# The second product of C11 in seven narrow products of its own, and k^T v in two halves through one buffer

## The chip, the cores and the metric

The kernel runs on one core of a Trainium2 chip. Its metric is the device time of one execution in microseconds. A run's time is compared with the median of three runs of the kernel before.

## The reference

An attention block without softmax, and then a feed-forward block with a squared ReLU, all in float32:

```python
# q, k, v: (8, 8, 576, 64)
kv  = einsum('bhsd,bhse->bhde', k, v)
out = einsum('bhsd,bhde->bhse', q, kv)
rms = sqrt(mean(out * out, axis=-1, keepdims=True) + 1e-6)
x   = (out / rms * g_norm).transpose(0, 2, 1, 3).reshape(4608, 512)
h   = x @ w_in                        # w_in (512, 2048)
r   = maximum(h, 0)
y   = (s * (r * r) + b) @ w_out       # w_out (2048, 512)
```

## The kernel before

The 4608 tokens are worked off in nine units u = 0 to 8 of 512 tokens. A unit is four chunks c of 128 tokens: the chunk's q is transposed (`turn`), multiplied by k^T v (`product`), normed (`norm`) and transposed back into xT (`turn_x`, 512 features in four blocks of 128 partitions, by 512 tokens).

**First product, x @ w_in.** For u >= 1 it is done by the Strassen-Winograd scheme at one level: features and tokens are each cut in two, so that a 2x2 block product takes seven products instead of eight. The blocks of the tokens' side are in xT (c, column halves of TB = 256 tokens) and their sums in `xs` (`x_sums`); those of the weights are in `wa`, `wb` and their sums in `ws` (`sums_w_in`). It is done in four steps s = 0 to 3; one step (`mm1(u, s)`) makes 256 columns of w_in by the upper and the lower half. Within a step the product i is four matmul calls (`mm1_product`: b over two blocks of 128 output features, c over two blocks of 128 input features), each of 256 token columns. In float32 a call is two PE instructions. The names say the product and the bank: x1, x6, x5, x3 are added up in one PSUM bank "x", y7 and y4 in a bank "y", z2 in a bank "z". C11 = product 1 + product 2: x1 is kept by ACT in r1 (line 569), and the DVE adds the bank of z2 to it (line 230) and squares its ReLU (line 524). C22 comes from x5 and y7 in the same way, x3 gives a21 (ReLU on ACT, line 600, square on DVE, line 603), y4 gives a12. The results, `ga`, are pairs of steps in one tile, `g_pair`, whose blocks the second product takes as weights.

**Second product, times w_out.** Unit 0 and 1 do it by one level of the scheme. From u = 2 on four of its products are done by a second level (`second_level`), again seven for eight, with matmuls of 128 columns; its banks are "x" or "y", "z" and "y", one tile each. Its weights come from DRAM into a ring of seven buffers, which `pump` fills by DMAs of SP (lines 645, 648).

**The order is written out by hand.** Each engine runs its instructions in the order in which the program names them. The slots of the steps are listed (x1 of a step, x3 of the step before, z2, y4 of the step before, x6, y7, x5), and beside certain slots stand other things: the sums of the weights of steps 1 to 3 in unit 1 (n = 1, 3, 5), k^T v of one batch (`kv_product`, units 1 to 6, n = 12), the load of the next k and v (`load_kv`, n = 14).

**Loads.** The DMAs of the units are issued by SP (but for two stores at the end). At the start of unit u, `loads(u)` issues the q of unit u + 1 (`load_q`: 34, 48, 32, 64, 48, 48, 32 DMAs in units 1 to 7, as a chunk's rows lie in one or two batches; line 155). `load_kv` (line 103) loads half of a batch's heads by four DMAs of 288 KB, two for k and two for v; both halves have a buffer of their own (bufs=2). `kv_product` (line 360) runs 144 instructions of 64x64 matmuls into two PSUM tiles kv_ps; four copies bring these to bd_kv (lines 373, 375).

PSUM has eight banks: two "t" (kv, transposes), one for the attention ("x" of ps_a), two "x", two "y", one "z". A bank holds 128 partitions by 512 float32 words, the whole of a tile [128, 2, 256].

Of the kernel before, what the change touches and what calls it, by code (L numbers as in the profile page):

```python
# [16 lines left out]
def kernel(  # L17
# [9 lines left out]
    moe_b: bass.AP,  # L27
    out: bass.AP,
):

# [211 lines left out]
    def sums_w_in(s):  # L244
# [12 lines left out]

        return s12, s34

    def w_in_of(i, s, b, c):  # L260
        return {
            1: lambda: wa[s][:, c, b],
            2: lambda: wa[s][:, KH + c, b],
            3: lambda: ws[s][:, 2, c, b],
            4: lambda: wb[s][:, KH + c, b],
            5: lambda: ws[s][:, 0, c, b],
            6: lambda: ws[s][:, 1, c, b],
            7: lambda: wb[s][:, c, b],
        }[i]()
# [75 lines left out]
        for _ in range(n):  # L345
            matmul(ps[:, 0, :P], ident, ident, True, True)

    def kv_product(b):


        ps = [ps_t.tile([P, 2, D], FP32, name="kv_ps", tag="t") for _ in range(2)]
        for i in range(2):
            if b == 0:
                warm((18, 7)[i])
            kv = kv_in.pop((b, i))
            for j in range(R):
                for l in range(2):
                    for r in range(2):
                        rows = slice(r * HB, r * HB + HB)
                        nc.tensor.matmul(  # L360
                            ps[r][l * HB : l * HB + HB, i, :],
                            lhsT=kv[rows, 0, l, j, :],
                            rhs=kv[rows, 1, l, j, :],
                            start=(j == 0),
                            stop=(j == R - 1),
                        )
        for r in range(2):
            for l in range(2):
                ls = slice(l * HB, l * HB + HB)
                to = bd_kv[b % 2][ls, 2 * r : 2 * r + 2, ls].rearrange("p i (c e) -> p i c e", c=KC)  # L370
                src = ps[r][ls].rearrange("p i (e c) -> p i c e", c=KC)
                if b == 0 and l == 1:
                    nc.vector.tensor_copy(out=to, in_=src)
                else:
                    nc.scalar.copy(to, src)
# [109 lines left out]
    def x_sums(u):  # L485
# [12 lines left out]

        return t12, t34

    def x_of(i, u, c):
        if i <= 3:
            c, col = (c, slice(0, TB)) if i == 1 else (KH + c, slice(0, TB) if i == 2 else slice(TB, 2 * TB))
            return xT[u][:, c, col]
        return xs[u, i][:, c, :]
# [5 lines left out]
    def bank_of(key, tag, bufs=2):  # L511
        bank[key] = ps_f.tile([P, 2, TB], FP32, name=f"{tag}_ps", tag=tag, bufs=bufs)
        return bank[key]

    def mm1_product(i, u, s, ps, first):
        for b in range(2):
            for c in range(KH):
                matmul(
                    ps[:, b, :], w_in_of(i, s, b, c), x_of(i, u, c),
                    first and b == 0 and c == 0, c == KH - 1,  # L520
                )
# [4 lines left out]
    def g_tile(name, s):  # L526
        if s % 2 == 0:
            g_pair[name, s // 2] = gp.tile([P, 2, 2, TB], FP32, name=name, tag=name)
        ga[name, s] = g_pair[name, s // 2][:, s % 2]
        return ga[name, s]  # L530
# [32 lines left out]
    def mm1(u, s):  # L563

        st = {}

        def keep(name, src, tag):
            st[name] = rp.tile([P, 2, TB], FP32, name=name, tag=tag)
            nc.scalar.copy(st[name], src)  # L569

        def x1():
            st["x"] = bank_of("x", "x")
            mm1_product(1, u, s, st["x"], True)
            keep("r1", st["x"], "ra")

        def z2():
            ps = bank_of("z", "z", 1)
            mm1_product(2, u, s, ps, True)
            t = g_tile("a11", s)
            add(t, ps, st["r1"])  # L580
            relu_sq(t)

        def x6():
            mm1_product(6, u, s, st["x"], False)
            keep("r2", st["x"], "rb")

        def y7():
            st["y"] = bank_of("y", "y")
            mm1_product(7, u, s, st["y"], True)

        def x5():
            mm1_product(5, u, s, st["x"], False)
            keep("r4", st["x"], "ra")
            t = g_tile("a22", s)
            add(t, st["y"], st["r4"])
            relu_sq(t)

        def x3():
            mm1_product(3, u, s, st["x"], False)
            nc.scalar.activation(g_tile("a21", s), st["x"], AF.Relu)  # L600

        def x3_square():
            nc.vector.tensor_mul(ga["a21", s], ga["a21", s], ga["a21", s])  # L603

        def x3_s1():
            g_tile("s1", s)
            g_s1(s)

        def x3_s3():
            sub(ga["a21", s], ga["a11", s], ga["a21", s])  # L610

        def y4():
            mm1_product(4, u, s, st["y"], False)
            add(g_tile("a12", s), st["y"], st["r2"])

        def y4_square():
            relu_sq(ga["a12", s])

        return dict(
            x1=x1, z2=z2, x6=x6, y7=y7, x5=x5, x3=x3, x3_square=x3_square, x3_s1=x3_s1,  # L620
            x3_s3=x3_s3, y4=y4, y4_square=y4_square,
        )

# [30 lines left out]
    def mm2(u, step=None, att=None):  # L656
# [281 lines left out]
            product_q[c]()  # L938
            norm[c]()

        def sums_ahead():
            p1["sums"]()
            turn[0]()
            turn[1]()

# [73 lines left out]
            y4_of(1, 4)  # L1019
            pump(2)  # L1020

        return sums_ahead, all_of_it


    NU = FC // 2
# [1 line left out]
    def tc_late():  # L1027
        convp.release()
        late["ring"] = ctx.enter_context(tc.tile_pool(name="ringp", bufs=7, side="right"))
        late["sub"] = ctx.enter_context(tc.tile_pool(name="subp", bufs=5, side="right"))  # L1030
        late["tmp"] = ctx.enter_context(tc.tile_pool(name="tmpp", bufs=4, side="right"))
        late["kv"] = ctx.enter_context(tc.tile_pool(name="kvp", bufs=2, side="right"))

    blocks = [i for s in range(NS) for i in (2 * s, NU + 2 * s)]
    blocks += [FC + 2 * s for s in range(2 * NS)]
# [91 lines left out]
    def side_of(u):  # L1127

        if u + 1 >= U:
            return None  # L1130
        turn, product, norm, turn_x, _ = zip(*(attention(c) for c in range(4 * u + 4, 4 * u + 8)))
        if u > 1:
            sums = lambda: [sums() for sums in x_sums(u + 1)]
            return turn, product, norm, turn_x, [sums]
        product = [whole(*steps) for steps in zip(product, norm)]
        side = {
            2: [turn[0]],
            3: [product[0]],
            4: [turn[1]],
            5: [turn_x[0], product[1]],  # L1140
            6: [turn[2]],
            7: [turn_x[1], product[2]],
            8: [turn[3]],
            9: [turn_x[2], product[3]],
            11: [turn_x[3]],
            12: [lambda: [sums() for sums in x_sums(u + 1)]],
        }
        if u == 0:
            side = {
                6: [lambda: kv_product(1)],  # L1150
                7: [turn[0]],
                8: [product[0], turn[1]],
                9: [turn_x[0], product[1], turn[2]],
                10: [turn_x[1], product[2], turn[3]],
                11: [turn_x[2], product[3]],
                12: [turn_x[3], lambda: [sums() for sums in sums_w_in(0)]],
                13: side[12],
            }
        return side
# [24 lines left out]
    for u in range(U):  # L1184
# [9 lines left out]
            for name in ("y4", "y4_square"):  # L1194
                a[name]()

        slots = []
        for s, a in enumerate(steps):
            slots.append(a["x1"])
            if s:  # L1200
                slots.append(partial(x3, steps[s - 1]))
            slots.append(a["z2"])
            if s:
                slots.append(partial(y4, steps[s - 1]))
            slots += [a["x6"], a["y7"], a["x5"]]
        if u == 0:
            first_unit()
        side = side_of(u)
        second = mm2(u, steps[-1], side) if u > 1 else mm2(u)
        for n, slot in enumerate(slots):  # L1210
            slot()
            if u > 1 and n == len(slots) - 2:
                second[0]()
            if u == 1 and n in (1, 3, 5):
                for sums in sums_w_in((n + 1) // 2):
                    sums()
            if u in kv_due and n == 12:
                kv_product(kv_due[u])
            elif u + 1 in kv_due and n == 14:
                for i in range(2):  # L1220
                    load_kv(kv_due[u + 1], i, late["kv"], tag="kv")
        if u > 1:
            second[1]()
            continue
        for n, slot in enumerate(second):
            slot()
# [18 lines left out]
                step()  # L1245
        if u == 0:
            tc_late()
            for i in range(2):
                load_kv(kv_due[1], i, late["kv"], tag="kv")
            pump(7)  # L1250


# [28 lines left out]
```

## Time and profile before

| what | value |
| --- | --- |
| runs | 952.93, 953.19, 955.08 us, median 953.19 |
| profiled execution | 956.6 us, of which the span of the core is 954.8 |
| granted TensorE clock | 0.997 of full |
| PE, DVE, ACT busy | 939.9 us (98%), 611.3 us (64%), 194.5 us (20%) |
| one unit, from u = 3 to 4 | 101.4 us (from 350.53 to 451.89 us) |
| z2 of all units | 256 instructions of 256 columns |
| kv_ps of all batches | 1152 instructions, 64x64 |
| HBM read and written | 125.8 and 24.1 MB |

The page calls an engine busy between the start and the end of an instruction. Matmuls are pipelined and their ends modelled, so the start of one group to the start of the next says what it costs. In the timeline the columns are start, duration, engine, line, operation, output tile and inputs, shapes and count, and in brackets the idle time of the engine just before and the instruction that ended it. PEld is the load of a matmul's weights, which runs beside the matmul before it. SPq is the issue of DMAs.

### The profile page before, as it was taken

What the parts mean: (1) busy time and instruction counts of PE and PEld (TensorE: products, weight loads), DVE (VectorE), ACT (ScalarE), POOL (GpSimd) and SP (SyncE); (2) the same over time, 40 slices, a digit from 0 to 9 for tenths busy, and PEclk for the clock granted to TensorE, in tenths of its full rate; (3) what the DMA queues carried; (4) which work ended last, traced back from release to release, by engine and by line L of the source; (5) the groups of instructions that cost most, each with busy time, mean ns of one, the idle gap of its engine ahead of it and who ended that gap; (6) DMA issues with size and microseconds to landing.
All of it is one profiled execution on the core that took longest, in us unless ns stands there. A gap on an engine that the chain in (4) does not pass through costs nothing.

```text
span 954.8 us, 17222 instructions
## 1 busy us (share of the span) xinstructions
PE 939.9 (98%) x7102; PEld 839.9 (88%) x7102; DVE 611.3 (64%) x1100; ACT 194.5 (20%) x366; POOL 6.7 (1%) x18
## 2 busy tenths in 40 slices
PE   6999999999999999999999999999999999999997
PEld 6888888888889998999889988989899989998997
DVE  1779768475447854686368744884478557864673
ACT  2674132211111112111211212121211111111100
POOL 2000000000000000000000000000000000000000
PEclk9999999999999999999999999999999999999999
DMA  9588929587735666365437554566225541662063
GB/s 216 192 310 230 309 69 260 107 249 253 210 69 140 181 189 138 76 201 159 128 81 200 185 159 84 159 197 181 32 81 180 184 87 42 202 176 68 20 223 100
DMA packets 131709, 151.09 MB, mean 158 GB/s; under 512 B 76592, under 2 KB 89136, under 8 KB 131504
## 3 DMA queue, kind: packets, MB, share of 16 engines
q1 hardware_dynamic: 128528, 148.22, 54.1%
q10 hardware_dynamic: 2784, 1.77, 0.8%
q8 instruction: 56, 0.92, 0.4%
q14 instruction: 21, 0.17, 0.1%
q0 software_dynamic: 320, 0.00, 0.0%
HBM read 125.83 MB, written 24.12 MB: 157 GB/s over the span
## 4 chain that ended last, share of the span: by engine, by line
PE 95%; DMA 2%; DVE 1%; ACT 1%; issue 0%; SPq 0%; ACTq 0%; DVEq 0%
PE x_ps L91 49%; PE y_ps L91 32%; PE z_ps L91 9%; PE x_ps L422 3%; PE kv_ps L360 2%; DMA w_raw<-in_moe_w_in_dram 1%; DMA kv_sb<-in_k_dram 1%; PE qT_ps L401 0%; DVE xn L441 0%; DVE xT L465 0%; ACT xT L471 0%; ACT w_raw L210 0%; ACT w_raw L205 0%; SPq L103 0%; DVE wb L225 0%
## 5 line engine op out<-in xcount | busy, mean ns | idle before, releaser
L91 PE MATMUL x_ps<-w_sb,a 128*128 128x256 f32 (+1 forms) x600 | 130.9, 371 | 0.0
L569 ACT COPY r<-x_ps 128x512 f32<-128x512 f32 x96 | 56.2, 585 | 332.4 <-PE x_ps L91 325.6
L91 PEld LDWEIGHTS x_ps<-w_sb,a 128*128 128x128 f32 x600 | 108.6, 190 | 15.2 <-issue 1.6
L91 PE MATMUL y_ps<-xs,wb 128*128 128x256 f32 x512 | 121.0, 379 | 0.0
L91 PE MATMUL x_ps<-xs,ws 128*128 128x256 f32 x512 | 120.9, 379 | 0.0
L230 DVE TENSOR_TENSOR a<-y_ps,r 128x512 f32<-128x512 f32 x64 | 44.1, 688 | 102.1 <-ACT r L569 96.4
L91 PEld LDWEIGHTS x_ps<-xs,ws 128*128 128x128 f32 x512 | 97.3, 190 | 13.2
L91 PEld LDWEIGHTS y_ps<-xs,wb 128*128 128x128 f32 x512 | 96.7, 190 | 12.9
L91 PE MATMUL x_ps<-xT,wa 128*128 128x256 f32 x384 | 89.6, 380 | 0.1
L91 PE MATMUL y_ps<-w_sb,sub 128*128 128x128 f32 x728 | 89.3, 275 | 0.0
L91 PEld LDWEIGHTS y_ps<-w_sb,sub 128*128 128x128 f32 x728 | 86.8, 192 | 1.3 <-DVE r L671 0.2
L91 PEld LDWEIGHTS x_ps<-xT,wa 128*128 128x128 f32 x384 | 72.3, 190 | 10.2 <-ACT xT L471 0.5
L91 PE MATMUL y_ps<-w_sb,a 128*128 128x128 f32 (+1 forms) x472 | 70.0, 294 | 0.0
L524 DVE SCALAR_TENSOR_TENSOR a<-a 128x512 f32<-128x512 f32 x96 | 66.4, 691 | 3.1
L91 PEld LDWEIGHTS y_ps<-w_sb,a 128*128 128x128 f32 x472 | 63.7, 191 | 4.1 <-issue 1.4
L603 DVE TENSOR_TENSOR a<-a 128x512 f32<-128x512 f32 x32 | 22.1, 689 | 61.0 <-ACT a L600 61.0
L91 PE MATMUL x_ps<-xT,ws 128*128 128x256 f32 x256 | 61.1, 382 | 0.0
L91 PE MATMUL z_ps<-xT,wa 128*128 128x256 f32 x256 | 60.5, 379 | 0.0
L91 PE MATMUL x_ps<-w_sb,s 128*128 128x256 f32 x256 | 59.1, 384 | 0.0
L91 PEld LDWEIGHTS x_ps<-w_sb,s 128*128 128x128 f32 x256 | 47.4, 190 | 8.4 <-issue 2.6
L91 PEld LDWEIGHTS z_ps<-xT,wa 128*128 128x128 f32 x256 | 48.6, 190 | 6.6
L91 PEld LDWEIGHTS x_ps<-xT,ws 128*128 128x128 f32 x256 | 47.6, 190 | 6.3
(126 smaller groups left out, 1060.4 us busy)
## 6 DMA issues: line engine op xcount, KB each, us to landing
w_sb<-w SPq DMA_DIRECT2D x140, 512.0 KB, 4.4
kv_sb<-in_k_dram SPq DMA_DIRECT2D x30, 288.0 KB, 4.8
kv_sb<-in_v_dram SPq DMA_DIRECT2D x30, 288.0 KB, 7.3
w_raw<-in_moe_w_in_dram SPq DMA_DIRECT2D x8, 1024.0 KB, 7.9
w_raw<-in_moe_w_out_dram SPq DMA_DIRECT2D x8, 1024.0 KB, 5.2
w_sb<-w SPq DMA_DIRECT2D x28, 256.0 KB, 2.8
out_dram<-o SPq DMA_DIRECT2D x104, 64.0 KB, 1.7
q_sb<-in_q_dram SPq DMA_DIRECT2D x144, 32.0 KB, 2.2
```

What stands on the lines that cost most here:

```text
L91: nc.tensor.matmul(o, lhsT=lhsT, rhs=rhs, start=start, stop=stop, skip_group_check=True)
L230: nc.vector.tensor_tensor(out=o, in0=a, in1=b, op=ALU.add)
L360: nc.tensor.matmul(ps[r][l * HB : l * HB + HB, i, :], lhsT=kv[rows, 0, l, j, :], rhs=kv[rows, 1, l, j, :], start=(j == 0), stop=(j == R - 1),)
L422: nc.tensor.matmul(ps[32 * p : 32 * p + 32, w, :], lhsT=st["qT"][:, p, 32 * w : 32 * w + 32], rhs=bd_kv[(b if w < 2 else b1) % 2][:, p, :] ...
L524: nc.vector.scalar_tensor_tensor(t, t, 0.0, t, ALU.max, ALU.mult)
L569: nc.scalar.copy(st[name], src)
L603: nc.vector.tensor_mul(ga["a21", s], ga["a21", s], ga["a21", s])
```

## The change

For u >= 1 product 2 of the first product (A12 B21, the z2 of two steps) is made by the scheme once more, over two steps d at a time: `mm1_twice` runs seven products of two matmul calls of 128 token columns, where z2 had four calls of 256 columns a step. x1 is copied by ACT straight into a11, and the seven results are added there by the DVE. Their banks "x" and "y" are the two halves of the z tile, "z" is a tile of ps_a. The sums for it are made from xT (`x21_sums`, for each unit) and from wa (`sums_w12`, once, partly in place). The order of the steps is written for pairs. `kv_product` is called for one half in the first pair of a unit and for the other in the second, and one buffer serves both: the second half is loaded after the product of the first, and the first half of the next batch after the product of the second. The turns of the first two q chunks (u > 1) come earlier, among the products of the second pair.

```diff
+    def sums_w12(s):
+        w12[s] = late["w"].tile([P, 3, P], FP32, name=f"w12_{s}")
+        s1, s2, s4 = (w12[s][:, i] for i in range(3))
+        add(s1, w12_at(s, 1, 0), w12_at(s, 1, 1))
+        sub(s2, s1, w12_at(s, 0, 0))
+        sub(w12_at(s, 1, 0), w12_at(s, 0, 0), w12_at(s, 1, 0))
+        sub(s4, w12_at(s, 0, 1), s2)
...
-    def kv_product(b):
...
-        ps = [ps_t.tile([P, 2, D], FP32, name="kv_ps", tag="t") for _ in range(2)]
-        for i in range(2):
+    def kv_product(b, halves=(0, 1)):
...
+        if halves[0] == 0:
+            kv_ps[b] = [ps_t.tile([P, 2, D], FP32, name="kv_ps", tag="t") for _ in range(2)]
+        ps = kv_ps[b]
+        for i in halves:
...
+        if halves[-1] == 0:
+            return
...
+    def x21_sums(u):
+        x21 = xs[u, 21] = late["w"].tile([P, 4, P], FP32, name="xs_21")
+        sub(x21[:, 0], x21_of(1, 2, u), x21_of(1, 1, u))
+        sub(x21[:, 1], x21_of(2, 2, u), x21[:, 0])
+        sub(x21[:, 2], x21_of(2, 2, u), x21_of(1, 2, u))
+        sub(x21[:, 3], x21_of(2, 1, u), x21[:, 1])
...
             mm1_product(1, u, s, st["x"], True)
-            keep("r1", st["x"], "ra")
-
-        def z2():
-            ps = bank_of("z", "z", 1)
-            mm1_product(2, u, s, ps, True)
-            t = g_tile("a11", s)
-            add(t, ps, st["r1"])
-            relu_sq(t)
+            nc.scalar.copy(g_tile("a11", s), st["x"])
...
+    def mm1_twice(u, d):
+
+        t = {}
+
+        def go(m, bank, first=False):
+            x = xs[u, 21][:, (5, 6, 7, 4).index(m)] if m > 3 else x21_of(*((1, 1), (2, 1), (2, 2))[m - 1], u)
+            for e in range(2):
+                matmul(t[bank][:, e], w12_of(m, 2 * d + e), x, first and e == 0, True)
+
+        def to(b, n, bank):
+            o = g_pair["a11", d][:, :, b, n * P : n * P + P]
+            add(o, o, t[bank])
+
+        def m1():
+            ps = bank_of("z", "z", 1)
+            t["x"], t["y"] = (ps[:, i].rearrange("p (e n) -> p e n", e=2) for i in range(2))
+            go(1, "x", True)
+            to(0, 0, "x")
+
+        def m2():
+            t["z"] = ps_a.tile([P, NP, P], FP32, name="z12_ps", tag="x")[:, :2]
+            go(2, "z", True)
+            to(0, 0, "z")
+
+        def m6():
+            go(6, "x")
+            to(1, 0, "x")
+
+        def m7():
+            go(7, "y")
+
+        def m5():
+            go(5, "x")
+            to(1, 1, "x")
+            to(1, 1, "y")
+
+        def m3():
+            go(3, "x")
+            to(0, 1, "x")
+
+        def m4():
+            go(4, "y")
+            to(1, 0, "y")
+            relu_sq(g_pair["a11", d].rearrange("p s b t -> p (s b t)"))
...
-        late["kv"] = ctx.enter_context(tc.tile_pool(name="kvp", bufs=2, side="right"))
+        late["w"] = ctx.enter_context(tc.tile_pool(name="latep", bufs=1, side="right"))
+        late["kv"] = ctx.enter_context(tc.tile_pool(name="kvp", bufs=1, side="right"))
...
-            sums = lambda: [sums() for sums in x_sums(u + 1)]
+            sums = lambda: [sums() for sums in (*x_sums(u + 1), lambda: x21_sums(u + 1))]
...
+        def kv_half(i):
+            kv_product(kv_due[u], (i,))
+            if i == 0:
+                load_kv(kv_due[u], 1, late["kv"], tag="kv")
+            elif u + 1 in kv_due:
+                load_kv(kv_due[u + 1], 0, late["kv"], tag="kv")
+
...
+        for d in range(NS // 2 if u > 0 else 0):
+            a, b = steps[2 * d : 2 * d + 2]
+            m = mm1_twice(u, d)
+            if u == 1 and d == 0:
+                x21_sums(1)
+                sums_w(1, 0, 1)
+            a["x1"]()
+            if d:
+                x3(steps[2 * d - 1])
+                y4(steps[2 * d - 1])
+            b["x1"]()
+            m[1]()
+            a["x6"]()
+            if d and u > 1:
+                second["turns"]()
+            m[2]()
+            m[6]()
+            a["y7"]()
+            m[7]()
+            m[5]()
+            a["x5"]()
+            if d == 0 and u == 1:
+                sums_w(2)
+            m[3]()
+            m[4]()
+            a["x3"]()
+            if u in kv_due:
+                kv_half(d)
+            for name in ("x3_square", "x3_s1", "x3_s3"):
+                a[name]()
+            y4(a)
+            if u == 1 and d == 0:
+                sums_w(3, 2, 3)
+            b["x6"]()
+            b["y7"]()
+            if d and u > 1:
+                second["sums"]()
+            b["x5"]()
...
-            for i in range(2):
-                load_kv(kv_due[1], i, late["kv"], tag="kv")
+            load_kv(kv_due[1], 0, late["kv"], tag="kv")
```

`sums_w(s, *more)` runs `sums_w_in(s)` and then `sums_w12` for each of `more`.

More of the change, by code (lines that the diff above doesn't have):

```diff
@@ L258, in sums_w_in, with w12_at, w12_of @@
         return s12, s34
+    w12 = {}
+    def w12_at(s, b, c):
+        return wa[s][:, KH + c, b]
+    def sums_w12(s):
[5 more added lines that the diff above has]
+        sub(s4, w12_at(s, 0, 1), s2)
+    def w12_of(m, s):
+        if m in (5, 6, 3):
+            return w12[s][:, (5, 6, 3).index(m)]
+        return w12_at(s, *{1: (0, 0), 2: (0, 1), 4: (1, 1), 7: (1, 0)}[m])
     def w_in_of(i, s, b, c):
@@ L346, in warm @@
             matmul(ps[:, 0, :P], ident, ident, True, True)
-    def kv_product(b):
-        ps = [ps_t.tile([P, 2, D], FP32, name="kv_ps", tag="t") for _ in range(2)]
-        for i in range(2):
+    kv_ps = {}
+    def kv_product(b, halves=(0, 1)):
[3 more added lines that the diff above has]
+        for i in halves:
             if b == 0:
@@ L499, in x_sums, with x21_of @@
         return t12, t34
+    def x21_sums(u):
[4 more added lines that the diff above has]
+        sub(x21[:, 3], x21_of(2, 1, u), x21[:, 1])
+    def x21_of(k, n, u):
+        return xT[u][:, KH + k - 1, n * P - P : n * P]
     def x_of(i, u, c):
@@ L619, in mm1 @@
         return dict(
-            x1=x1, z2=z2, x6=x6, y7=y7, x5=x5, x3=x3, x3_square=x3_square, x3_s1=x3_s1,
+            x1=x1, x6=x6, y7=y7, x5=x5, x3=x3, x3_square=x3_square, x3_s1=x3_s1,
             x3_s3=x3_s3, y4=y4, y4_square=y4_square,
         )
+    def mm1_twice(u, d):
[32 more added lines that the diff above has]
+            relu_sq(g_pair["a11", d].rearrange("p s b t -> p (s b t)"))
+        return {1: m1, 2: m2, 3: m3, 4: m4, 5: m5, 6: m6, 7: m7}
     ring = {}
@@ L939, in attend, with turns @@
             norm[c]()
-        def sums_ahead():
-            p1["sums"]()
+        def turns():
             turn[0]()
@@ L1020, in all_of_it @@
             pump(2)
-        return sums_ahead, all_of_it
+        return {"turns": turns, "sums": p1["sums"], "rest": all_of_it}
     NU = FC // 2
@@ L1145, in side_of @@
             11: [turn_x[3]],
-            12: [lambda: [sums() for sums in x_sums(u + 1)]],
+            12: [lambda: [sums() for sums in x_sums(u + 1)], lambda: u and x21_sums(u + 1)],
         }
@@ L1195, in y4, with sums_w @@
                 a[name]()
[L1197 to L1205, printed above, removed]
+        side = side_of(u)
+        second = mm2(u, steps[-1], side) if u > 1 else mm2(u)
+        def sums_w(s, *more):
+            for sums in sums_w_in(s):
+                sums()
+            for s in more:
+                sums_w12(s)
@@ L1206 @@
+        def kv_half(i):
[4 more added lines that the diff above has]
+                load_kv(kv_due[u + 1], 0, late["kv"], tag="kv")
         if u == 0:
             first_unit()
[L1208 to L1219, printed above, removed]
-                for i in range(2):
-                    load_kv(kv_due[u + 1], i, late["kv"], tag="kv")
+        for d in range(NS // 2 if u > 0 else 0):
[36 more added lines that the diff above has]
+            b["x5"]()
@@ L1222 @@
         if u > 1:
-            second[1]()
+            second["rest"]()
             continue
@@ L1247 @@
             tc_late()
-            for i in range(2):
-                load_kv(kv_due[1], i, late["kv"], tag="kv")
+            load_kv(kv_due[1], 0, late["kv"], tag="kv")
             pump(7)
```

## The prediction

> **What bounds the kernel now.** I read the page's busy times first, then the waits of TensorE (PE), then the timeline in the units u >= 1, where all of the change but its first load lies.
>
> ```profile
> PE   939.9 (98%) x7102; PEld 839.9 (88%) x7102; DVE 611.3 (64%) x1100; ACT 194.5 (20%) x366; POOL 6.7 (1%) x18
> ...
> PE 95%; DMA 2%; DVE 1%; ACT 1%; issue 0%; SPq 0%; ACTq 0%; DVEq 0%
> ```
>
> PE is the bound, and the list of its waits holds 2.0 us of waiting for kv data and some single waits in unit 0: from unit 1 on, PE has no gap. So every column of matmul that is saved counts in full, and so does every new wait of PE. The price of a column comes from the starts of consecutive groups (durations overlap, starts do not):
>
> ```profile
> 296.52 1.05 PE L91 MATMUL x_ps<-w_sb,a 128*128 128x128 f32 x8
> 297.41 1.06 PE L91 MATMUL z_ps<-w_sb,a 128*128 128x128 f32 x8
> ...
> 350.53 1.89 PE L91 MATMUL x_ps<-xT,wa 128*128 128x256 f32 x8
> 352.26 1.89 PE L91 MATMUL z_ps<-xT,wa 128*128 128x256 f32 x8
> 353.99 1.89 PE L91 MATMUL x_ps<-xs,ws 128*128 128x256 f32 x8
> ```
>
> Four calls (eight instructions) of 256 columns take 1.73 us, four of 128 columns 0.89 us. The narrow ones cost 0.1116 us an instruction against half of 0.2158: 3% worse per column.
>
> **1. The second product.** It goes from 2 x 1.727 = 3.454 us a pair of steps to 7 products x 4 instructions x 0.1116 = 3.125 us: 0.329 saved, 16 pairs (8 units, 2 each): **-5.3 us**. Were narrow columns as cheap as wide ones it would be -6.9.
>
> **2. m3, then m4.** In the new helper the halves "x" and "y" are one PSUM tile, one bank. m3 writes "x", the DVE adds it into a11, and m4 writes "y" right behind m3 with nothing between. Does PE have to wait with m4 until the DVE has read the other half? Nothing in this trace writes a bank beside a reader of it: the second-level products of mm2 keep x, y and z in three banks. The nearest row is unit 0's kv_ps, of which each tile is read by ACT (lower partitions) and by DVE (upper partitions):
>
> ```profile
> 14.01 0.42 ACT L375 COPY bd_kv<-kv_ps 64x128 f32<-64x128 f32 x2 [11.99 <-PE kv_ps L360]
> 14.29 0.50 DVE L373 COPY bd_kv<-kv_ps 64x128 f32<-64x128 f32 x2 [13.26 <-ACT bd_kv L375]
> ```
>
> The DVE had nothing else to do and started 0.02 us after the first ACT copy's 0.26 us, and its releaser is that copy: two readers of disjoint parts of one tile were put in order. (They also write one SBUF tile, so the row does not prove that PSUM was the reason.) I take it that a PSUM tile is ordered as a whole. The Trainium skill, "PSUM — Partial Sum Buffer", section "PSUM bank collisions raise a hardware error", says that two engines on one bank and the same partitions collide even at disjoint columns, so that m4 would have to wait; no run here shows the collision. By that page the term below is the whole 37.6, by the reading that only bytes count it is 0.
>
> The price: before m3's add the DVE has the add and the square of x5, and these wait for ACT's copy of x5.
>
> ```profile
> 371.25 1.89 PE L91 MATMUL x_ps<-xT,wa 128*128 128x256 f32 x8
> 371.51 0.59 ACT L569 COPY r<-x_ps 128x512 f32<-128x512 f32 x1 [2.92 <-PE x_ps L91]
> 372.12 0.69 DVE L230 TENSOR_TENSOR a<-y_ps,r 128x512 f32<-128x512 f32 x1 [3.88 <-ACT r L569]
> 372.85 0.69 DVE L524 SCALAR_TENSOR_TENSOR a<-a 128x512 f32<-128x512 f32 x1
> ```
>
> From the end of x5 (371.25) the square starts at 1.60. An independent operation starts 0.61 after a square (187.07 to 187.68 in unit 1), so m3's add runs from 2.21, for about 0.42 (rows of 128x256 adds: 0.41), to 2.63. PE starts about 0.15 after a DVE end (25.94 to 26.63 and 19.26 to 19.95 were followed at 0.06 and 0.15). So m4 starts at 2.78 instead of 0.45: 2.33, taken as 2.35, x 16 = **+37.6 us**. Bounds: 0 if halves are tracked apart, 2.75 a pair (44) if the weight load (0.19) waits too and the add takes 0.48 like the PSUM rows of that size. I take the middle because the row favours order. What is queued behind m4 is all of PE; late next are only DVE's m4 add and the 1024-wide square, which fit under x3 and y4 (3.45 us). The other bank orders are covered: m6 to m7 has y7 between (1.73 against 0.2 + 0.42 + 0.15), m5 to m3 has x5 (1.73 against about 1.25). ACT's a11 copies replace the r1 copies one for one. In all, DVE's extra adds and sums go under PE at 64% busy, except as follows.
>
> **3. The sums at unit 1.** In unit 1 the DVE ends x_sums at about 147.9, PE starts x1 at 144.66. Now four x21 sums (128 wide, 0.9 us from the slope of the 512 and 256 rows), sums_w_in(1) (4 x 0.61 + 0.1 = 2.5) and two w12 (0.9 each) stand ahead of m1's add: 147.9 + 5.3 + 0.45 = 153.7. PE gets to m6 after x1, x1, m1, x6, m2: 150.7. **+3.1**. sums_w(2) comes between x5's square and m3's add: **+2.4**. sums_w(3) finds slack. Bounds 3 to 9 (the upper: x1 of unit 1 must wait for the in-place sums of wa).
>
> **4. kv in halves.** kv_product costs 275.80 - 269.89 - 2 x 1.727 = 2.46 us of which 144 instructions are 2.26: 0.20 for going in and out. Done twice a unit, in 6 units: **+1.2**. More costly is its load. The second half's four DMAs are now issued by SP in the first pair, behind loads(u), the q pieces of the next unit:
>
> ```profile
> 458.51 34.80 SPq L155 DMA_DIRECT2D q_sb<-in_q_dram  x64
> 493.41 1.26 SPq L103 DMA_DIRECT2D kv_sb<-in_k_dram  x2
> 494.71 1.25 SPq L103 DMA_DIRECT2D kv_sb<-in_v_dram  x2
> ```
>
> Unit 4 starts at 451.89, so SP is free at +41.5; 1.18 MB land some 6.2 later (8 loads move 1.06 MB in the first 5.6 us there): +47.8, or +48.6 if x21_sums (0.8 on the DVE ahead of the stores) delays SP. PE wants the second half at 18 products x 1.727 + 2 x 3.125 + 1.33 = +38.7, with the waits of 2 at +43.4: 4.4 to 5.2, taken as **+4.8**, in unit 4. The q queues end at +39.9, +32.2, +24.6, +35.5, +33.4 in units 1, 2, 3, 5, 6, where the half lands before PE comes. Nothing else is late: the first half has a unit's time. The turns moved ahead are DVE work of 1.3 us under x6, their q pieces landed by then.
>
> **5. Clock.** PE's wait of 3.75 us in unit 0 (to 24.45) is followed by a granted clock of 0.88 and 0.70 in the two 4 us stretches from 22 to 30, a loss of 4 x 0.12 + 4 x 0.30 = 1.7 us. Two of the new gaps are longer (unit 1's m4 wait 4.8, unit 4's kv 4.8): **+3.4**. Bounds 0, and 16 x 1.7 = 27 if the 2.35 us gaps did it as well. The Trainium skill, "TensorE: Matmul & The Clock Gate", section "What's actually happening", puts the drop at an idle window of about 3.4 us; by it the 2.35 us gaps cost nothing and the sum stands, where the row alone allows the 27.
>
> Sum: -5.3 + 37.6 + 3.1 + 2.4 + 1.2 + 4.8 + 3.4 = **+47.2 us**. The profiled execution took 956.6 us (span 954.8), its sum 1003.8; the median of the runs is 953.2, 3.4 lower, hence **1000.4 us**. Own range 988 to 1012 (the ends of 2, 3 and 4).
>
> **Rivals.**
> A, halves tracked apart (no wait at m4). Then the kv load decides: PE is at +38.9 at the second half. Unit 4 waits 9.3 (48.2 - 38.9), unit 5 3.3, unit 6 1.2, unit 1 0.4 behind DVE delays of 4.2 (3.1, and 1.1 where r2's copy waits for y4's add); x3 waits 0.1 for r4's copy, 16 times. -5.3 + 1.2 + 14.2 + 4.2 + 1.6 + 1.7 for one long gap's clock = +17.6: **971 us**. For it: no row with PE and DVE on one bank. Against: the kv_ps row.
> B, the 2.35 us gaps lower the clock each time: 15 gaps more than in part 5, x 1.7: +47.2 + 25.5 = **1026 us**. Against: unit 0 only shows it for 3.75 us.
> C, faster: the saved columns win. Place: the 16 pairs; price -5.3 + 1.2 = -4.1, **949 us**. It decides if the added waits stay below 0.26 us a pair (4.1/16), so SP must also bring the second half by +38.7 in unit 4, nine microseconds sooner than its queue is free plus a landing. Against it stands q x64 ahead of kv, word for word above.
> D, the saving eats the waits and nothing moves: as C, with 4 us of waits left in all, 953.
>
> **Chances.** Forecast 0.84, A 0.08, B 0.04, C 0.025, D 0.015. The forecast's own range holds nine in ten of it, 0.76; to hold eight in ten, with some room in A's direction, I give 985 to 1014. About 0.3% (2.9 us) is what a measurement of this kernel tells from no change: faster 0.025, same 0.015, slower 0.96.
>
> **What would show it.** Right: PE waits for DVE of about 2.3 us, 16 times, ahead of the "y" matmuls of the z tile; PE waits for DMA kv_sb once, in unit 4; 448 instructions of 128 columns at 0.11 us for the second product; PE's share down to some 95%. Wrong: m4 starting 0.45 after m3 (A), a granted clock of 0.8 or less in all units (B), no PE wait for kv_sb in unit 4 (the load is not behind q).

## The result, and the profile after

The changed kernel takes 1011.75 us (median, 1006.05 to 1015.58), the kernel before 954.59 (median of six) in the same comparison: a ratio of 1.0592, 95% interval 1.0555 to 1.0630. 1000.4 was forecast, in a range of 985 to 1014. The profiled execution took 1008.21 us (span 1006.4), 51.6 us more than the profiled one of before.

The page after, busy times and chain:

```profile
PE 952.4 (95%) x7294; PEld 851.4 (85%) x7294; DVE 645.4 (64%) x1212; ACT 194.9 (19%) x366; POOL 6.7 (1%) x18
...
PE 86%; DVE 5%; DMA 3%; SPq 3%; ACT 1%; issue 1%; ACTq 0%; DVEq 0%
```

PE is still busy for most of the span, but the chain that ended last now goes through DVE, DMA and SP's queue for 11% where it was 3%. What it goes through stands in the list of PE's waits (who waited for whom: us in total, times, longest):

```profile
PE z_ps L92 <- DVE a L231: 38.0, 17, 4.5
PE kv_ps L384 <- DMA kv_sb<-in_v_dram: 5.2, 4, 3.3
```

Of the 17, sixteen stand ahead of m4 and one ahead of unit 1's m6. Of the 5.2 us for kv, 4.0 are in unit 4, the rest in unit 0. The list of before has no row of the first kind, and for kv, in unit 0 alone:

```profile
PE kv_ps L360 <- DMA kv_sb<-in_v_dram: 2.0, 3, 0.9
```

One pair of unit 3 in the timeline:

```profile
374.29 1.89 PE L92 MATMUL x_ps<-xs,ws 128*128 128x256 f32 x8
...
376.02 0.61 PE L92 MATMUL z_ps<-xT,w 128*128 128x128 f32 x4
376.22 0.59 ACT L606 COPY r<-x_ps 128x512 f32<-128x512 f32 x1 [4.65 <-PE x_ps L92]
376.83 0.69 DVE L231 TENSOR_TENSOR a<-y_ps,r 128x512 f32<-128x512 f32 x1 [1.47 <-ACT r L606]
377.56 0.69 DVE L561 SCALAR_TENSOR_TENSOR a<-a 128x512 f32<-128x512 f32 x1
378.17 0.41 DVE L231 TENSOR_TENSOR a<-a,z_ps 128x256 f32<-128x256 f32 x1
...
378.64 0.71 PE L92 MATMUL z_ps<-xs,wa 128*128 128x128 f32 x4 [2.01 <-DVE a L231]
```

The rows are, in order, x5, m3, ACT's copy of x5, the DVE's add and square of x5, the DVE's add of m3 (378.17 to 378.58), and 0.06 us later m4, which writes the other half of the tile. From m3 to m4 it is 2.62 us instead of 0.45.

Unit 4, where the second half of kv comes late:

```profile
478.83 33.95 SPq L156 DMA_DIRECT2D q_sb<-in_q_dram  x64
512.88 1.26 SPq L104 DMA_DIRECT2D kv_sb<-in_k_dram  x2
...
514.12 1.89 PE L92 MATMUL x_ps<-xT,ws 128*128 128x256 f32 x8
519.28 0.44 PE L384 MATMUL kv_ps<-kv_sb 64*64 64x64 f32 x2 [3.27 <-DMA kv_sb<-in_v_dram]
520.47 2.19 PE L384 MATMUL kv_ps<-kv_sb 64*64 64x64 f32 x70 [0.74 <-DMA kv_sb<-in_v_dram]
```

SP is busy with 64 pieces of q until 512.8, PE would have begun the half at 515.95 and begins its bulk at 520.47. Those 70 instructions then take 2.19 us where the half of unit 3 takes 1.28, because of the clock (columns: stretch, length, busy time and instructions of PE, PEld, DVE, ACT, POOL, granted clock, DMA share, GB/s):

```profile
161.00:165.00 4.00, 3.25 (x10) 2.81 (x11) 2.34 (x4) 0.00 (x0) 0.00 (x0) 0.50 0.49 95
...
484.00:488.00 4.00, 3.69 (x11) 3.15 (x12) 1.91 (x3) 0.00 (x0) 0.00 (x0) 0.57 0.34 52
...
520.00:524.00 4.00, 3.53 (x73) 3.21 (x74) 0.00 (x0) 1.04 (x4) 0.00 (x0) 0.50 0.00 0
```

The first and the last follow the two long waits; the middle one follows an ordinary wait for m4 of 2.01 us (484.31). Two more such stretches are at 836 and 914, each behind an ordinary wait for m4 of 2.0 to 2.1 us. Between the starts of units (first x1 to first x1, in unit 8 to the end of the span) the time went so:

| unit | before, us | after, us | more | what is in it |
| --- | --- | --- | --- | --- |
| 1 | 104.51 | 116.86 | 12.35 | two waits at m4, one of them 2.5 longer; m6 3.0; half clock |
| 2, 3, 5, 6, each | 101.36 | 105.67 | 4.31 | two waits at m4 |
| 4 | 101.36 | 114.15 | 12.79 | two waits at m4; kv 4.5; half clock |
| 7 | 98.90 | 104.52 | 5.62 | two waits at m4; half clock |
| 8 | 99.9 | 105.6 | 5.6 | two waits at m4; half clock |

Unit 1 starts 2.0 us earlier than before: in unit 0 PE waits 1.9 us for ACT's work on the weights w_raw, where it waited 3.7 in the profiled run of before. The sum is 51.6.

### The profile page after: what moved, and what is told of

It reads as the page before. It is cut to its first block, busy times and chain, and to the rows that moved or that the text cites. A ratio compares the mean times of both kernels' runs of the same rounds, so it can differ in the third digit from the quotient of the medians.

```text
span 1006.4 us, 17699 instructions
## 1 busy us (share of the span) xinstructions
PE 952.4 (95%) x7294; PEld 851.4 (85%) x7294; DVE 645.4 (64%) x1212; ACT 194.9 (19%) x366; POOL 6.7 (1%) x18
## 4 chain that ended last, share of the span: by engine, by line
PE 86%; DVE 5%; DMA 3%; SPq 3%; ACT 1%; issue 1%; ACTq 0%; DVEq 0%
PE x_ps L92 44%; PE y_ps L92 29%; PE z_ps L92 7%; PE x_ps L448 3%; SPq L156 3%; PE kv_ps L384 2%; DVE a L231 1%; DMA w_sb<-w 1%; DMA w_raw<-in_moe_w_in_dram 1%; DVE a L561 1%; DMA kv_sb<-in_k_dram 1%; ACT r L606 1%; DVE xs L234 1%; DMA kv_sb<-in_v_dram 1%; DVE ws L234 0%
## 5 line engine op out<-in xcount | busy, mean ns | idle before, releaser
L92 PE MATMUL y_ps<-xs,wb 128*128 128x256 f32 x512 | 123.6, 385 | 0.0
L231 DVE TENSOR_TENSOR a<-a,z_ps 128x256 f32<-128x256 f32 x112 | 47.1, 420 | 90.2 <-PE z_ps L92 66.3
L92 PEld LDWEIGHTS x_ps<-xs,ws 128*128 128x128 f32 x512 | 94.8, 190 | 11.6
L606 ACT COPY r<-x_ps 128x512 f32<-128x512 f32 x64 | 37.5, 586 | 204.2 <-PE x_ps L92 204.2
L92 PE MATMUL x_ps<-xT,ws 128*128 128x256 f32 x256 | 66.1, 405 | 0.0
L561 DVE SCALAR_TENSOR_TENSOR a<-a 128x512 f32<-128x512 f32 (+1 forms) x80 | 63.8, 798 | 2.5
L92 PEld LDWEIGHTS x_ps<-xT,ws 128*128 128x128 f32 x256 | 51.0, 207 | 6.9
L92 PE MATMUL z_ps<-xs,wa 128*128 128x128 f32 x128 | 22.9, 306 | 35.2 <-DVE a L231 35.2
L92 PEld LDWEIGHTS z_ps<-xs,wa 128*128 128x128 f32 x128 | 19.4, 205 | 39.1 <-DVE a L231 38.2
```

The source lines that it names most:

```text
L92: nc.tensor.matmul(o, lhsT=lhsT, rhs=rhs, start=start, stop=stop, skip_group_check=True)
L231: nc.vector.tensor_tensor(out=o, in0=a, in1=b, op=ALU.add)
L561: nc.vector.scalar_tensor_tensor(t, t, 0.0, t, ALU.max, ALU.mult)
```

## Experiments

**Is it the shared bank?** "y" is put into the free half of m2's tile; the DVE's order stays.

```diff
-            t["x"], t["y"] = (ps[:, i].rearrange("p (e n) -> p e n", e=2) for i in range(2))
+            t["x"] = ps[:, 0].rearrange("p (e n) -> p e n", e=2)
...
-            t["z"] = ps_a.tile([P, NP, P], FP32, name="z12_ps", tag="x")[:, :2]
+            ps = ps_a.tile([P, NP, P], FP32, name="z12_ps", tag="x")
+            t["z"], t["y"] = ps[:, :2], ps[:, 2:]
```

> Only the place of "y" changes: it becomes the free half of m2's tile in ps_a, so m3 and m4 write different banks. Theory (a PSUM tile is ordered as a whole, so m4 waits for the DVE's read of m3): the sixteen waits of 2.0 to 4.5 us ahead of m4 go, 16 x 2.3 + 2.4 = 39 us less, and PE then comes 4.6 us earlier to the second half of kv and waits longer for it: about 9 us in unit 4, 3 in unit 5, 1 in unit 6. Unit 1's wait at m6 (2.8 us) stays. Time 968 to 976 us, 1.4 to 2.3% over the kernel before. Rival (the DVE is late whatever the bank, and the wait moves to the next matmul that needs it): within 10 us of the changed kernel's 1012.

Measured: 977.97 us against 952.99, ratio 1.0265 (1.0248 to 1.0282). PE's waits, and unit 4 in the timeline:

```profile
PE kv_ps L384 <- DMA kv_sb<-in_v_dram: 15.5, 8, 9.4
PE z_ps L92 <- DVE a L231: 2.8, 1, 2.8
...
490.30 0.61 PE L92 MATMUL z_ps<-xT,w 128*128 128x128 f32 x4
490.74 0.61 PE L92 MATMUL z_ps<-xs,wa 128*128 128x128 f32 x4
491.19 1.99 PE L92 MATMUL x_ps<-xT,ws 128*128 128x256 f32 x8
502.62 0.44 PE L384 MATMUL kv_ps<-kv_sb 64*64 64x64 f32 x2 [9.43 <-DMA kv_sb<-in_v_dram]
```

m4 follows m3 at 0.44 us, in every pair. All sixteen waits are gone with the sharing, and 32 of the 57 us. More than half of what is left are waits for kv, 14.5 us in units 4 to 6: PE comes earlier and waits 9.4 us in unit 4, 2.3 in unit 5. The time is 2 us above the range that was expected. That wait was expected at 9, but not that the clock stays at 0.5 until 509, long after PE has begun again at 502.6:

```profile
497.00:501.00 4.00, 0.00 (x0) 0.00 (x0) 0.00 (x0) 0.00 (x0) 0.00 (x0) 0.50 0.92 215
501.00:505.00 4.00, 1.62 (x46) 1.50 (x50) 0.00 (x0) 0.00 (x0) 0.00 (x0) 0.50 0.38 80
505.00:509.00 4.00, 4.00 (x45) 3.34 (x38) 0.00 (x0) 1.04 (x4) 0.00 (x0) 0.50 0.37 97
```

**Is it the work that stands before m3's add?** The bank stays shared; x5's add and square are named after m3's add.

```diff
             keep("r4", st["x"], "ra")
+
+        def x5_add():
             t = g_tile("a22", s)
             add(t, st["y"], st["r4"])
             relu_sq(t)
...
             a["x5"]()
+            m[3]()
+            a["x5_add"]()
             if d == 0 and u == 1:
                 sums_w(2)
-            m[3]()
             m[4]()
...
             b["x5"]()
+            b["x5_add"]()
```

> The bank of "y" stays shared; only the DVE's order changes: the add of m3 comes ahead of the add and the square of x5. Theory (m4 waits for the read of m3, which stands behind 1.4 us of other DVE work): the gap from the end of m3 to m4 falls from 2.2 us to about 0.8 (0.2 to the DVE's start, 0.42 the add, 0.15 back), 16 x 1.4 = 22 us less, and sums_w(2) in unit 1 no longer counts (2.4); with fewer drops of the clock 980 to 990 us. Rival (m4 waits for the square of x5 or for another thing than m3's read): the gap stays above 2 us.

Measured: 979.37 us, ratio 1.0281 (1.0265 to 1.0296).

```profile
PE z_ps L92 <- DVE a L231: 11.0, 17, 2.8
...
366.69 0.61 PE L92 MATMUL z_ps<-xT,w 128*128 128x128 f32 x4
366.89 0.59 ACT L606 COPY r<-x_ps 128x512 f32<-128x512 f32 x1 [4.65 <-PE x_ps L92]
367.34 0.42 DVE L231 TENSOR_TENSOR a<-a,z_ps 128x256 f32<-128x256 f32 x1 [1.30 <-PE z_ps L92]
...
367.81 0.71 PE L92 MATMUL z_ps<-xs,wa 128*128 128x128 f32 x4 [0.51 <-DVE a L231]
```

m4 still waits for exactly this add, but the wait is 0.51 us, not 2.01: each wait falls by 1.5 and the total by 27. The time is 0.6 us below the range that was expected, although PE comes earlier here too and waits 7.1 us for kv in unit 4; behind none of the waits of 0.5 us does the granted clock fall. The two runs together show the two parts of the term: which read m4 waits for (that of the other half of its tile), and how late that read is (what the DVE has before it). The bank experiment changes the tile and the bank of "y" at once, so whether the order goes by the tile or by the bank is not shown, and that the chip would fail without this order was not tried.

**Is the kv half late through SP's order?** The second q load goes behind the load of the second half.

```diff
             load_q(4 * u + 4)
-            load_q(4 * u + 6)
+            if u not in kv_due:
+                load_q(4 * u + 6)
...
                 load_kv(kv_due[u], 1, late["kv"], tag="kv")
+                load_q(4 * u + 6)
```

> Only SP's order changes: in the units with kv, the second load of q is issued after the load of the second half of kv. Theory (the second half is late because SP issues up to 64 q pieces first): PE's wait for kv in unit 4 (4.0 us, with 6.8 us at half clock behind it) goes, 5 to 8 us less than the changed kernel. Rival (the load is late by its own landing time or by bandwidth): the wait in unit 4 stays, no change of time.

Measured: 1004.30 us, ratio 1.0533 (1.0512 to 1.0555), some 6 us less than the changed kernel, each against its own runs of before (give or take 4, as the changed kernel's runs scatter). In unit 4 SP issues the half at 490.5, behind 16 pieces of q instead of 64, and PE waits there for DVE only:

```profile
480.94 8.43 SPq L156 DMA_DIRECT2D q_sb<-in_q_dram  x16
490.53 1.71 SPq L104 DMA_DIRECT2D kv_sb<-in_k_dram  x2
...
PE z_ps L92 <- DVE a L231: 4.1, 2, 2.1
```

**What do the waits cost through the clock?** Dummy matmuls, which nothing reads, are run during the wait.

```diff
-            t["z"] = ps_a.tile([P, NP, P], FP32, name="z12_ps", tag="x")[:, :2]
+            t["ps"] = ps_a.tile([P, NP, P], FP32, name="z12_ps", tag="x")
+            t["z"] = t["ps"][:, :2]
...
         def m4():
+            for _ in range(9):
+                matmul(t["ps"][:, 2], ident, x21_of(1, 1, u), False, True)
             go(4, "y")
```

> Nine dummy calls of 128 columns (18 instructions, 2.0 us) are put between m3 and m4, into columns of m2's tile that nothing reads, so PE works through the wait. Theory (the gaps of 2 us also lower the clock, now and then): the waits of DVE shrink to some 0.1 us, the granted clock goes from 0.98 to 0.99 or more, and the time falls by 5 to 10 us though PE does 32 us more of work. Rival (only the gaps over 3.7 us lower the clock, and the rest of the scatter has another cause): same time within 3 us.

Measured: 1002.74 us, ratio 1.0523 (1.0507 to 1.0539), granted clock 0.995 in the profile against 0.985.

```profile
372.90 0.61 PE L92 MATMUL z_ps<-xT,w 128*128 128x128 f32 x4
373.34 2.17 PE L92 MATMUL z_ps<-xT,ident 128*128 128x128 f32 x18
375.52 0.71 PE L92 MATMUL z_ps<-xs,wa 128*128 128x128 f32 x4
```

m4 is at 2.62 us behind m3, as without the dummies, and yet the kernel is about 7 us faster (49.8 over its kernel before, not 57.2; give or take 4). In this profile the clock falls to half only behind unit 1's m6 and at the wait for kv in unit 4, and behind none of the sixteen places of m4. So some 7 us are what these waits cost over and above their length; they are not the ordinary waits alone, for the dummies also shorten unit 1's wait of 4.5 us at m4 to 2.5. The granted clock of the changed kernel's runs goes roughly with their time: 0.988 in the fastest (1006.05 us), 0.981 in the slowest (1015.58).

**Both large edits together.** The edits of the first and the third experiment.

> Both edits together: "y" in m2's tile, and the second load of q behind the load of the second half of kv. Theory (these two waits, with the clock they cost, are all but some 5 us of the loss): left over are -5.3 for the columns, +1.2 for going twice into kv, 16 x 0.1 where x3 waits for ACT's copy of x5, and 3 to 6 us in unit 1: 954 to 959 us, within 0.6% of the kernel before, granted clock 0.995 or more. Rival (a further cost, such as ACT's copies into a11 or the narrow matmuls themselves, sits in every unit): 965 or more.

Measured: 956.34 us against 953.15, ratio 1.0034 (1.0022 to 1.0046), granted clock 0.997. No cost of the size that the rival named sits in the units. What is left of PE's waits behind unit 0:

```profile
PE z_ps L92 <- DVE a L231: 2.8, 1, 2.8
...
PE x_ps L92 <- ACT r L606: 0.7, 1, 0.7
```

**With the sums of unit 1 ordered by when they are due.** On top of both:

```diff
-        sub(w12_at(s, 1, 0), w12_at(s, 0, 0), w12_at(s, 1, 0))
+        sub(s3, w12_at(s, 0, 0), w12_at(s, 1, 0))
...
                 x21_sums(1)
-                sums_w(1, 0, 1)
+                sums_w12(0)
+                sums_w12(1)
...
             m[5]()
+            if u == 1:
+                sums_w(2 * d + 1)
             a["x5"]()
-            if d == 0 and u == 1:
-                sums_w(2)
             m[3]()
             m[4]()
-            a["x3"]()
             if u in kv_due:
                 kv_half(d)
+            a["x3"]()
...
-                sums_w(3, 2, 3)
+                sums_w12(2)
+                sums_w12(3)
...
             b["x5"]()
+            if u == 1 and d == 0:
+                sums_w(2)
```

> As the run with both edits, and besides in unit 1 the weights' sums are ordered by when they are due (w12 not in place, sums_w_in(1) behind m5, sums_w_in(2) behind the pair, sums_w_in(3) in the second pair), and the half of kv comes before x3, which gives ACT's copy of x5 1.3 us. Theory: no PE wait over 1 us is left behind unit 0; -5.3 + 1.2 + about 1 = -3 us, 949 to 952 us, 0.2 to 0.4% faster than the kernel before. Rival (the saved columns are eaten by something that these edits do not touch): 954 or more.

Measured: 951.41 us, ratio 0.9978 (0.9968 to 0.9988): 0.2% faster than the kernel before. The wait at m6 is down to 0.3 us:

```profile
PE z_ps L92 <- DVE a L231: 0.3, 1, 0.3
```

Its unit 2 takes 101.06 us (247.43 to 348.49) against 101.36 before: 0.30 less, where two pairs' saving less one way into kv should give 0.46. Unit 7, which has no kv, shows the saving by itself: it takes 98.41 us here (752.71 to 851.12) and in the run with both edits, against 98.90 before. That is 0.49 less where two pairs were reckoned at 0.66.

**The halves alone.** The kernel before with kv in halves, the first beside n = 7 and the second beside n = 20, the second q load behind the load of the second half.

> The kernel before, with kv in halves through one buffer alone (first half beside n = 7, second beside n = 20, the second load of q behind the load of the second half); the second product stays z2. Theory (the price of the halves, once their load is in time, is going in and out of the 64x64 matmuls twice): 6 x 0.20 = +1.2 us, 0.1%, and no wait of PE for kv. Rival (a half in time costs more than that, by waits or by the DMAs' place): +3 us or more.

Measured: 954.90 us against 953.15, ratio 1.0016 (1.0007 to 1.0025), which is +1.75 us, with 0.7 to 2.4 for the interval. The +1.2 lies inside it, the rival's 3 outside. PE has no wait for kv from unit 1 on. A unit with kv, 2 to 6, takes 101.71 us against 101.36 (347.47 to 449.18 in unit 3), so that going in and out once more costs 0.35 here, not 0.20. The version with all edits is 3.5 us faster than this one (951.41 against 954.90): so much the seven products brought, with the order of their sums.

## Why the prediction was right, point by point

- **The bound, and the saved columns (-5.3).** PE had no gap, so each new wait counted. The narrow matmuls run at 0.1116 us an instruction, as reckoned (0.446 for m1's four, 146.08 to 146.52). The saving is there but smaller: 0.49 us in unit 7 of the two versions without gaps, about 3.9 in eight units, where 5.3 was reckoned. In that unit the product behind m4, x3, takes 1.78 and 1.83 us to the next start instead of 1.73, which is most of the difference. Rival A had this as a wait for ACT's copy; the cause is not shown.
- **m4 (+37.6).** Right in place, in cause and in size: 2.33 reckoned from four rows, 2.17 to 2.23 measured from m3's end to m4's start, and 0.1 more behind it, as m4's group takes 0.55 instead of 0.45. The add starts as reckoned (2.15 us behind x5's end, against 2.21), and PE follows its end at 0.06 instead of 0.15. The kv_ps row was a weak witness, as the prediction said; the two experiments on the bank and on the DVE's order are the proof. The Trainium skill, "PSUM — Partial Sum Buffer", section "PSUM bank collisions raise a hardware error", asks for this order; the runs show the order and its price, not the collision.
- **Unit 1's sums (+3.1, +2.4).** m6 starts at 151.69 where 148.70 was free: 3.0. m4 starts at 161.75, 2.5 later than in the other pairs. Both as reckoned (the parts of the first sum add up to 5.2, not 5.3).
- **kv (+1.2, +4.8).** The one way more was measured at 1.75 alone. Unit 4 waits 4.5, the other units not, as reckoned; that the size came out is in part luck, for both sides of the difference are later than reckoned: PE is at the half 45.1 us into the unit instead of 43.4, and has its last data at 49.6 instead of 47.8 to 48.6. In the bank experiment the waits reckoned for rival A came out: 9.4 in unit 4.
- **The clock (+3.4), the term that was too small.** The step took a loss of 1.7 us for two long gaps only and nothing for gaps of 2.3. In the profile, unit 1 loses about 2.5, unit 4 about 4.0 (12.79 - 4.31 - 4.5), units 7 and 8 about 1.7 each, some 10 in all. Half of it, three times 1.7, stands behind ordinary gaps; the two long ones take the rest, some 4.8 instead of 3.4. The dummies bear it out: some 7 us go when the gaps at m4 are filled. So the clock is 6 to 7 of the 10 us between 47.2 and 57.2. Between the medians the loss is 5.6 more than between the two profiled runs; 2.0 of that is the profiled run of before, which lies above its median, and the rest is the scatter of the changed kernel's runs. The range was built from the ends of points 2, 3 and 4 and had no room for this; that it holds the result, 2 us below its end, is in part luck. The Trainium skill, "TensorE: Matmul & The Clock Gate", section "What's actually happening", with its idle window of about 3.4 us, gives nothing for a wait of 2.01 us; the stretch at 484 to 488 with its clock of 0.57 says otherwise, and the measurement decides.
- **The rivals.** A (halves apart) fell with the two runs on the bank; its price, 971, was 7 below the run that makes it true, for the clock again. B (every gap lowers the clock) was wrong as put, but three of the ordinary gaps in the profile did. C and D needed the waits hidden, and these were not; with the waits taken away, 951.4 is left of C's 949.

## What to carry to other kernels

Where TensorE has no gap, saving 0.33 us of columns by seven narrow products for two wide ones was lost many times over at one place, where two accumulators of consecutive products share a bank: put two accumulators into one bank only if other matmuls stand between the read of one and the next write of the other. In the bank experiment "y" still shares a bank, with "z", but m6 and y7 stand between, and PE does not wait. What a wait costs is then read from the reader's queue: the add took 0.4 us, the work queued before it 1.4. And when a buffer is halved, ask what its later load is now queued behind: 64 pieces of 8 to 32 KB held the issuing queue for 34 us.

## What the runs showed of the hardware that was not expected

A TensorE wait of 2.0 us can be followed by some 3.4 us at a granted clock of one half (484.31 and on: m4's group takes 0.94 us to the next start instead of 0.55), but most such waits are not: three of the fifteen ordinary ones in the profile, and five of fifteen in the profile with the later q load (behind 191.06, 273.78, 830.03, 908.40 and 936.27). The wait of 2.8 us at m6 is not followed by it in the changed kernel's profile, and is followed by it in each of the five others that have that wait. What decides it is not shown. The time of the kernel scatters with it: 1006 to 1016 us with clocks of 0.988 to 0.981, where the kernel before stays within 5 us. With the wait of 9.4 us the clock was at 0.50 from within the wait until 509, 6.4 us after PE had begun again.
